# Fewer accumulating transfers and a re-ordered first step in a linear-attention and feed-forward kernel

## The chip, the core and the metric

The kernel runs on one core of a Trainium2 chip. The time is device microseconds of one execution, as a median over executions. The core has TensorE (matrix products into PSUM), VectorE, ScalarE and GpSimd (elementwise work), SyncE, which here only issues transfers, and 16 DMA engines that all queues share. SyncE's queue is SP in the profile, VectorE is DVE, GpSimd is POOL, ScalarE is ACT, TensorE is PE.

## What is computed

A gated linear attention over 4 sequences, 8 heads, 768 positions and head size 48, followed by a feed-forward layer (384 to 2048 to 384) with a piecewise quadratic activation:

```python
f = 1.0 / (1.0 + np.exp(-f_logit))
for t in range(S):
    state = f[:, :, t, :, None] * state + np.einsum('bhd,bhe->bhde', k[:, :, t], v[:, :, t])
    y[:, :, t] = np.einsum('bhd,bhde->bhe', q[:, :, t], state)
h = x @ w_in                    # x: y as 3072 tokens of 384
g = np.where(h >= 1, h, np.where(h <= -1, 0.0, (h + 1) ** 2 / 4))
out = g @ w_out
```

The weights arrive in double precision (`in_w`, two 32-bit words per number).

## The kernel before, in words

**Attention.** The 768 positions are cut into six steps of 128. In each step the eight heads are four pairs; pairs 0 to 2 fill 128 partitions together with a third each of pair 3's rows, so three tiles of keys, queries and gates are loaded and pair 3's tile is gathered from them by six moves (`move`, SBUF to SBUF, alternately issued by SP and ScalarE). `gate` turns the gate logits of one tile into running products: a sigmoid on ScalarE, then on VectorE two scans, a clamp (`end`), a reciprocal and two products with keys and queries, and a small product (`pf`, line 409) of 128x4 numbers, the decay of the state; GpSimd copies that on. For each pair, `scores` makes the products of keys and queries of four sequences in two PSUM banks; VectorE multiplies both banks with the causal mask (`am`, line 456); `outputs` multiplies with the values, and from step 1 on adds the state's part. ScalarE then copies the outputs in rounded form (`hi`, line 511), and VectorE writes what the rounding left (`lo`, line 512). Pair 3's outputs go by six moves (`x<-y`) into the tiles of pairs 0 to 2, since the feed-forward layer wants all 384 features of a position in three tiles. `transpose_tensor` turns the keys on TensorE, ScalarE copies them (`kn`, line 472), and `states` makes the step's part of the state. In steps 2 to 4 VectorE turns the keys instead (`transpose_rows`).

**Feed-forward.** 96 units: 16 slices of 128 hidden features for each of six steps. `unit_1` is nine matmuls (lines 204: three tiles, each with the weights' `lo` and `hi` times `x` hi, and `hi` times `x` lo), then ScalarE, ScalarE and VectorE for the activation (lines 208, 211, 216), ScalarE for its rounded part `ghi` (219), VectorE for the rest `glo` (222). `unit_2` is nine matmuls (228) into three banks that collect 16 units. TensorE's order is unit u+1's first product, then attention work if there is some, then unit u's second product.

**Weights.** 24 pieces of 128x512 (six per quarter: three of `w_in`, three of `w_out`; `k` numbers them). VectorE builds a float from the two words in three instructions (306, 309, 311). Then ScalarE writes the negative rounded value into `w_lo` (315), GpSimd issues a transfer that adds the exact value to it in SBUF (316, an accumulating transfer), and ScalarE writes `w_hi` (317). Units 0 to 3 need the first quarter, units 4 to 7 the second, and so on. Later 24 checks (325) load every piece once more.

**What sets the order.** The program lists operations with engine, estimated cost and dependencies (`Plan.add`); `Plan.order` is a list scheduler: each engine takes the ready operation with the earliest due time. TensorE's operations are chained in the order in which they are listed. The instructions are then written out in that order, and where the plan sees TensorE idle for over 700 ns it puts matmuls of zeros (`warm`, line 282) there. Each engine carries out its instructions in that fixed order. Transfers are given one of eight completion semaphores in turn, and an issue waits until the earlier transfer on its semaphore has landed.

Of the kernel before, what the change touches and what calls it, by code (L numbers as in the profile page):

```python
# [21 lines left out]
C = 128  # L22
NI = S // C
NP = H // 2
# [113 lines left out]
def gla_moe(ctx: ExitStack, tc: tile.TileContext, ff, kqd, f0, vv, wd, maskd, identd, gates, values, headsd, out):  # L138
# [8 lines left out]
    zeros = const.tile([128, 512], BF16, name="zeros")  # L147
# [5 lines left out]
    v = tiles(3, [C, B, 2, D], F32, "v")  # L153
# [18 lines left out]
    ident = const.tile([C, C], F32, name="ident")  # L172

# [14 lines left out]
    def whole(t):  # L188
        return t[:, 2 * N:]
# [89 lines left out]
    def warm(count):  # L279
        for _ in range(count):  # L280
            if opened["bank"] is not None:
                nc.tensor.matmul(opened["bank"], zeros[:, 0:128], zeros, start=opened["start"], stop=opened["start"])
# [14 lines left out]
    def split_piece(k):  # L297
# [69 lines left out]
    def gate(m):  # L367
# [41 lines left out]
        c["pf"] = [vec("small", lambda: nc.vector.tensor_tensor(out=whole(t), in0=et, in1=f0s[:, g:g + B], op=ALU.mult),  # L409
# [3 lines left out]
    def elementwise(n):  # L413
# [7 lines left out]
        c["lv"] = dma(v[n % 3], vv[i, p], 192, old(n - 3, "y", "st"))  # L421
# [18 lines left out]
    def scores(n):  # L440
# [11 lines left out]
        c["sc"] = add("PE", "scores", emit, c["kq"], [d for h in held for d in h[2]])  # L452
        c["am"] = []
# [8 lines left out]
    def transpose_tensor(n):  # L462
        i, p = pairs[n]
        c = att[n]
        b, ps, held = bank(i == 0)
# [21 lines left out]
    def outputs(n):  # L487
# [6 lines left out]

        def emit():
            for m in range(B):

                vb = v[n % 3][:, m].rearrange("u h e -> u (h e)")
                nc.tensor.matmul(ps[0:64, m], vb[:, 0:64], ms[0][:, m], start=True, stop=first)  # L499
                nc.tensor.matmul(ps[64:R, m], vb[:, D:], ms[1][:, m], start=True, stop=first)  # L500
# [5 lines left out]
        c["y"] = add("PE", "y0" if first else "y", emit, c["am"], c["lv"], c["db"], held)  # L506
# [5 lines left out]
        el = vec("dve", lambda: nc.vector.tensor_tensor(out=lo[:R], in0=yf[:R], in1=hi[:R].bitcast(F32), op=ALU.subtract), eh)  # L512
        banks[b] = [eh, el]
# [6 lines left out]
    def states(n):  # L520
# [4 lines left out]
        b, ps, held = bank(i == 0)  # L525
# [3 lines left out]
        def emit():  # L529
            for m in range(B):  # L530
                for h, (r, z) in enumerate(rows):
                    nc.tensor.matmul(ps[r:z, m, :D], kn[n % 2][:, B - 1 - m, r:z], v[n % 3][:, m, h], start=True, stop=True)
# [85 lines left out]

    for n in range(NP):
# [11 lines left out]
    BY_TENSOR = 2  # L631
# [7 lines left out]
    for u in range(NI * NJ):  # L639
        unit_1(u)  # L640
        for kind, n in sorted(groups.get(u, [])):
            if kind == 0:
# [3 lines left out]
                scores(n)  # L646
            else:
# [141 lines left out]
```

## Time and profile before

| | |
|---|---|
| median of 3 runs | 528.28 us (527.29 to 529.44) |
| profiled execution | 527.07 us, span of the program 525.3 us |
| TensorE busy | 500.1 us, 95% of the span, granted clock 0.986 |
| VectorE busy | 387.3 us, 74% |
| ScalarE busy | 243.6 us, 46% |
| GpSimd busy | 30.8 us, 6% |
| accumulating transfers (queue q0) | 24, 6.29 MB, 6.8% of the DMA engines' span |
| hardware queue of SP (q1) | 51.31 MB, 30.5% |

A busy TensorE in the profile is no TensorE at its peak, since matmuls overlap; nine matmuls of 128x512 that follow each other start over 2.04 us. The prediction reads the stages, the waits and the chain of waits; all times in it count from the span's start. A row of waits names the engine, its tile and line, and what ended its idle time.

### The profile page before, as it was taken

To read this page: it belongs to the slowest core of one execution; us is meant where nothing else is said; L and a number is where in the kernel's file an instruction comes from. 1 tells how busy PE (TensorE), PEld (TensorE's weight loads), DVE (VectorE), ACT (ScalarE), POOL (GpSimd) and SP (SyncE) were. 2 spreads that over 40 slices of the span, in tenths; PEclk is the share of its full clock that TensorE was granted. 3 is DMA by queue.
4 is the path that set the end of the run, shared out by engine and by line. 5 is a ranking of instruction groups with operands and counts; after the bars stand their busy time and mean duration, and the time that the engine had idled before them with its cause. 6 is when DMAs were issued, how large, how long until landed. Compare 5 with 4: busy or idle time off the path is not lost.

```text
span 525.3 us, 8288 instructions
## 1 busy us (share of the span) xinstructions
PE 500.1 (95%) x3226; PEld 404.0 (77%) x3226; DVE 387.3 (74%) x775; ACT 243.6 (46%) x399; POOL 30.8 (6%) x54
## 2 busy tenths in 40 slices
PE   8765998999999999999999999999999999999995
PEld 4433887788778888788888888888888888888883
DVE  7866998999999999898898798865655443433332
ACT  3334776664443544434434434534443544444542
POOL 1121221310000000000000000000000000000000
PEclk9996999999999999999999999999999999999998
DMA  8699988985311113322115423044542211100001
GB/s 297 211 294 243 242 226 221 281 203 134 109 51 55 35 62 87 119 103 100 60 57 132 129 72 116 23 148 119 176 131 92 80 41 31 61 1 0 1 0 66
DMA packets 24526, 60.57 MB, mean 115 GB/s; under 512 B 3744, under 2 KB 7328, under 8 KB 24480
## 3 DMA queue, kind: packets, MB, share of 16 engines
q1 hardware_dynamic: 19872, 51.31, 30.5%
q0 software_dynamic: 3456, 6.29, 6.8%
q10 hardware_dynamic: 1152, 2.37, 1.9%
q8 instruction: 27, 0.44, 0.3%
q14 instruction: 19, 0.16, 0.1%
HBM read 44.22 MB, written 4.72 MB: 93 GB/s over the span
## 4 chain that ended last, share of the span: by engine, by line
PE 71%; DVE 17%; DMA 7%; issue 2%; ACT 2%; ACTq 0%; SPq 0%; DVEq 0%
PE po L228 31%; PE ph L204 30%; DMA f<-in_f 3%; PE pa L450 3%; DMA x<-y 2%; PE pa L504 2%; PE pa L500 2%; DVE glo L222 2%; DVE kn L483 2%; DVE am L456 2%; DVE w L393 2%; DVE act L216 2%; DVE bits L311 1%; DVE f L400 1%; DMA raw<-in_w 1%
## 5 line engine op out<-in xcount | busy, mean ns | idle before, releaser
L204 PE MATMUL ph<-x,w_hi 128*128 128x512 f32 x576 | 179.1, 392 | 0.0
L208 ACT ACTIVATE act<-ph,half 128x512 f32<-128x512 f32 x96 | 66.0, 687 | 142.1 <-PE ph L204 136.1
L204 PEld LDWEIGHTS ph<-x,w_hi 128*128 128x128 f32 x576 | 109.4, 190 | 22.8
L204 PE MATMUL ph<-x,w_lo 128*128 128x512 f32 x288 | 113.3, 394 | 9.8 <-DMA x<-y 9.4
L228 PE MATMUL po<-ghi,w_lo 128*128 128x512 f32 x288 | 115.6, 401 | 1.3 <-ACT ghi L219 1.3
L216 DVE SCALAR_TENSOR_TENSOR act<-ph,act 128x512 f32<-128x512 f32 x96 | 65.8, 686 | 64.7 <-ACT act L211 63.6
L228 PE MATMUL po<-ghi,w_hi 128*128 128x512 f32 x288 | 112.4, 390 | 0.0
L219 ACT CAST ghi<-act 128x512 fp32r<-128x512 f32 x96 | 59.5, 620 | 81.7 <-DVE act L216 81.5
L228 PE MATMUL po<-glo,w_hi 128*128 128x512 f32 x288 | 83.3, 391 | 0.5 <-DVE glo L222 0.5
L222 DVE TENSOR_TENSOR glo<-act,ghi 128x512 fp32r<-128x512 f32 x96 | 65.9, 686 | 22.3 <-ACT ghi L219 21.2
L204 PEld LDWEIGHTS ph<-x,w_lo 128*128 128x128 f32 x288 | 54.7, 190 | 22.2 <-issue 9.9
L228 PEld LDWEIGHTS po<-ghi,w_lo 128*128 128x128 f32 x288 | 54.0, 188 | 15.2 <-ACT ghi L219 2.6
L228 PEld LDWEIGHTS po<-glo,w_hi 128*128 128x128 f32 x288 | 53.9, 188 | 13.2 <-DVE glo L222 1.8
L228 PEld LDWEIGHTS po<-ghi,w_hi 128*128 128x128 f32 x288 | 54.1, 188 | 10.4
L211 ACT ACTIVATE act<-act 128x512 f32<-128x512 f32 x96 | 60.7, 632 | 3.0
L483 DVE STREAM_TRANSPOSE kn<-kq 32x128 f32<-32x128 f32 x192 | 58.1, 303 | 2.9
L456 DVE TENSOR_TENSOR am<-pa,mask 128x512 f32<-128x512 f32 x43 | 29.3, 685 | 17.6 <-PE pa L450 13.9
L499 PE MATMUL pa<-am,v 128*64 128x128 f32 x184 | 35.5, 279 | 1.4 <-ACT kn L472 0.9
L500 PE MATMUL pa<-am,v 128*48 128x128 f32 x184 | 34.5, 277 | 0.5 <-DVE am L456 0.5
L503 PE MATMUL pa<-kq,dbd 112*64 112x128 f32 x160 | 30.6, 272 | 0.0
L504 PE MATMUL pa<-kq,dbd 112*48 112x128 f32 x160 | 30.6, 272 | 0.0
L450 PEld LDWEIGHTS pa<-kq 48*128 48x128 f32 x344 | 21.3, 187 | 6.6 <-issue 4.9
(79 smaller groups left out, 454.4 us busy)
## 6 DMA issues: line engine op xcount, KB each, us to landing
raw<-in_w SPq DMA_DIRECT2D x48, 512.0 KB, 3.7
kq<-in_kq SPq DMA_DIRECT2D x18, 512.0 KB, 4.2
w_lo<-bits POOLq DMA_DIRECT2D x24, 256.0 KB, 6.9
v<-in_v SPq DMA_DIRECT2D x24, 192.0 KB, 4.3
out_y<-raw SPq DMA_DIRECT2D x18, 256.0 KB, 2.3
f<-in_f SPq DMA_DIRECT2D x16, 256.5 KB, 3.0
kq<-kq SPq DMA_DIRECT2D x18, 64.2 KB, 3.3
kq<-kq ACTq DMA_DIRECT2D x18, 64.2 KB, 3.5
```

The source lines that it names most:

```text
L204: nc.tensor.matmul(ps, w_in(part, j, kt), xt[:, kt, t], start=(n == 0), stop=(n == 8))
L208: nc.scalar.activation(a, ps, AF.Relu, bias=half, scale=0.5)
L211: nc.scalar.activation(a, a, AF.Square)
L216: nc.vector.scalar_tensor_tensor(out=a, in0=ps, scalar=1.0, in1=a, op0=ALU.max, op1=ALU.min)
L219: nc.scalar.copy(hi, a)
L222: nc.vector.tensor_tensor(out=lo, in0=a, in1=hi.bitcast(F32), op=ALU.subtract)
L228: nc.tensor.matmul(po[e], w_out(part, j, e), g, start=(j == 0 and n == 0), stop=(j == NJ - 1 and n == 2))
L450: nc.tensor.matmul(ps[:, b], kt[a:z, B - 1 - b], qt[a:z, b], start=True, stop=True)
L456: o = vec("dve", lambda t=t, ps=ps: nc.vector.tensor_tensor(out=t, in0=ps, in1=mask.rearrange("u (o t) -> u o t", o=1).broadcast_to([C, B, ...
L483: nc.vector.transpose(kn[n % 2][u:u + 32, :, r:r + 32], src[:, :, u:u + 32])
L500: nc.tensor.matmul(ps[64:R, m], vb[:, D:], ms[1][:, m], start=True, stop=first)
L504: nc.tensor.matmul(ps[64:R, m], dt[:, m, 64:R], qt[:, m], start=False, stop=True)
```

## The change

1. *Weights.* Only pieces with odd `k` from 7 on (nine) are still made by an accumulating transfer. For the other fifteen ScalarE writes `w_hi` first and VectorE subtracts it from the value (new line 323).
2. *Step 0.* Scores of the next pair are listed ahead of a pair's outputs, and the masks (`masks`) apart from the scores. All outputs come ahead of the turned keys: pairs 0 and 1 are turned after the last remainder, pairs 2 and 3 after unit 1 (lines 480, 564). 
3. *Step 0's remainders.* Each output product is made in two banks (lines 514 and 521); a matmul with a negative unit matrix (`minus`, line 540) subtracts the rounded copy from the second one, and ScalarE writes the remainder from there (541). VectorE's instruction stays for steps 1 to 5 (544 and 545).
4. *Decays.* The small product `pf` is GpSimd's (415).
5. *Fillers and costs.* Ahead of unit 0 the zero matmuls fill the whole planned gap and four more are added; the tile of zeros is 128x128 and read four times; some planning costs differ; the values have four buffers instead of three.

```diff
-HOP, LANDING, PER_KB, NEAR = 200, 2000, 3.0, 2000
-COST = dict(mm=227, scores=1100, y0=1050, y=1850, states=500, turn=500, rows=317, scan=1145, dve=605, small=200, state=365,
-            words=430, act=710, copy=530, sig=540, issue=480, near=600, least=300, swdge=1000)
+HOP, LANDING, PER_KB, NEAR = 200, 2000, 3.0, 2700
+COST = dict(mm=227, scores=1100, y0=1850, y=1850, states=500, turn=500, rows=317, scan=1145, dve=605, small=200, state=365,
+            words=390, act=710, copy=530, sig=540, issue=480, near=600, least=300, swdge=900)
...
-        n = sca("copy", lambda: nc.scalar.activation(w_lo[:, c], val, AF.Copy, scale=-1.0), v)
-        l = add("POOL", "swdge", lambda: nc.gpsimd.dma_start(w_lo[:, c], val, accum_op=ALU.add), n, near=True)
-        h = sca("copy", lambda: nc.scalar.copy(w_hi[:, c], val), v)
+        if k >= 6 and k % 2:
+
+            n = sca("copy", lambda: nc.scalar.activation(w_lo[:, c], val, AF.Copy, scale=-1.0), v)
+            l = add("POOL", "swdge", lambda: nc.gpsimd.dma_start(w_lo[:, c], val, accum_op=ALU.add), n, kb=560)
+            h = sca("copy", lambda: nc.scalar.copy(w_hi[:, c], val), v)
+        else:
+            h = sca("copy", lambda: nc.scalar.copy(w_hi[:, c], val), v)
+            l = vec("dve", lambda: nc.vector.tensor_tensor(out=w_lo[:, c], in0=val, in1=w_hi[:, c].bitcast(F32), op=ALU.subtract), h)
...
-        c["pf"] = [vec("small", lambda: nc.vector.tensor_tensor(out=whole(t), in0=et, in1=f0s[:, g:g + B], op=ALU.mult),
+        c["pf"] = [add("POOL", "least", lambda: nc.gpsimd.tensor_tensor(out=whole(t), in0=et, in1=f0s[:, g:g + B], op=ALU.mult),
...
+        again = bank(True) if first else None
...
+                else:
+                    for r, z, a, t in ((0, 64, 0, ms[0]), (64, R, D, ms[1])):
+                        nc.tensor.matmul(again[1][r:z, m], vb[:, a:a + z - r], t[:, m], start=m == 0, stop=False)
...
-        el = vec("dve", lambda: nc.vector.tensor_tensor(out=lo[:R], in0=yf[:R], in1=hi[:R].bitcast(F32), op=ALU.subtract), eh)
-        banks[b] = [eh, el]
+        c["rest"] = b, again, yf[:R], hi[:R], lo[:R], eh
+        if not first:
+            remainder(n)
+
+    def remainder(n):
+
+        i, p = pairs[n]
+        b, again, yf, hi, lo, eh = att[n]["rest"]
+        xt = x[i % 2]
+        if again:
+            y = wide(again[1])[:R]
+            o = add("PE", 300, lambda: nc.tensor.matmul(y, minus, hi, start=False, stop=True), eh, ready["minus"])
+            el = sca("act", lambda: nc.scalar.copy(lo, y), o)
+            banks[b], banks[again[0]] = [eh], [el]
+        else:
+            el = vec("dve", lambda: nc.vector.tensor_tensor(out=lo, in0=yf, in1=hi.bitcast(F32), op=ALU.subtract), eh)
+            banks[b] = [eh, el]
...
     for n in range(NP):
         prepare(n)
-        if n == 0:
-            ready["ident"] = dma(ident, identd, 64)
         scores(n)
-        outputs(n)
-        transpose_tensor(n)
-        states(n)
+        if n > 0:
+            outputs(n - 1)
+        if n > 1:
+            remainder(n - 2)
+        masks(n)
+    outputs(NP - 1)
+    remainder(NP - 2)
+    remainder(NP - 1)
+    for n in (0, 1):
+        transpose_tensor(n, True)
+    for n in (0, 1):
+        states(n, True)
...
     for u in range(NI * NJ):
         unit_1(u)
+        if u == 1:
+            for n in (2, 3):
+                transpose_tensor(n)
+            for n in (2, 3):
+                states(n)
...
-                if idle and o.start - idle > 700:
+                if o is unit_in[0, 0]:
+
+                    warm(int((o.start - idle) / 230) + 4)
+                elif idle and o.start - idle > 700:
```

TensorE at the end of step 0 and ahead of unit 0, before (`kq_71` holds pair 3's keys, `kn` turned keys, `ph` the units' banks):

```order
L500 MATMUL po_118<-am_79,v_72 48x128
L469 MATMUL pa_111<-ident,kq_71 128x112 x4
L282 LDWEIGHTS zeros
...
L532 MATMUL pa_112<-v_72,kn_82 64x48
...
L282 MATMUL ph_115<-zeros 128x512
L204 MATMUL ph_114<-x_88,w_lo 128x512
```

and with the change (`y_91` holds pair 3's rounded outputs):

```order
L521 MATMUL po_118<-am_79,v_75 64x128
...
L540 MATMUL po_118<-y_91,minus 112x512
L480 MATMUL po_119<-ident,kq_68 128x112 x4
L480 MATMUL po_120<-ident,kq_69 128x112 x4
...
L564 MATMUL pa_114<-v_73,kn_83 48x48
...
L283 MATMUL ph_117<-zeros 128x512
L205 MATMUL ph_116<-x_89,w_lo 128x512
```

Pairs 0 and 1 are now turned where pair 3 was, behind the last remainder; ten zero matmuls stood between the states and unit 0, and eleven do now.

SP around the moves of pair 3's outputs, before (`raw` are pieces of the weights):

```order
L241 DMA kq_69<-in_kq 128x1024
L241 DMA raw_95<-in_w 128x512
L241 DMA kq_70<-in_kq 128x1024
L241 DMA raw_96<-in_w 128x512
L241 DMA raw_97<-in_w 128x512
L241 DMA v_74<-in_v 128x384
L241 DMA raw_95<-in_w 128x512
L241 DMA v_72<-in_v 128x384
L246 DMA x_88<-y_90 16x1024 x3
```

and with the change:

```order
L242 DMA raw_96<-in_w 128x512
L242 DMA raw_97<-in_w 128x512
L242 DMA raw_98<-in_w 128x512
L242 DMA raw_96<-in_w 128x512
L242 DMA kq_68<-in_kq 128x1024
L247 DMA x_89<-y_91 16x1024 x3
L242 DMA raw_97<-in_w 128x512
L242 DMA kq_69<-in_kq 128x1024
```

Two of step 1's three loads of keys and queries, and its values, now stand behind the moves; seven pieces of the weights stand ahead of them in both.

VectorE ahead of unit 6's third activation step, before:

```order
L311 SCALAR_TENSOR_TENSOR bits_100<-raw_97,bits_100 128x512
L396 TENSOR_SCALAR end_77<-w 128x4
L399 RECIPROCAL rec<-end_77 128x4
L400 SCALAR_TENSOR_TENSOR f_66<-f_66,rec 128x512
L402 TENSOR_TENSOR kq_70<-kq_70,w 128x512
L404 TENSOR_TENSOR kq_70<-kq_70,f_66 128x512
L456 TENSOR_TENSOR am_80<-pa_112,mask 128x512
L512 TENSOR_TENSOR x_89<-pa_113,x_89 112x512
L216 SCALAR_TENSOR_TENSOR act_86<-ph_114,act_86 128x512
```

and with the change:

```order
L313 SCALAR_TENSOR_TENSOR bits_101<-raw_98,bits_101 128x512
L399 SCALAR_TENSOR_TENSOR w<-f_66,ones 128x512
L323 TENSOR_TENSOR w_lo<-bits_99,w_hi 128x512
L323 TENSOR_TENSOR w_lo<-bits_101,w_hi 128x512
L402 TENSOR_SCALAR end_78<-w 128x4
L405 RECIPROCAL rec<-end_78 128x4
L406 SCALAR_TENSOR_TENSOR f_66<-f_66,rec 128x512
L217 SCALAR_TENSOR_TENSOR act_87<-ph_116,act_87 128x512
```

The two products and the mask have moved behind the step, and two of the new weight remainders stand ahead of it. From the start to this step VectorE's list has 15 pieces in both, 11 weight remainders instead of none, no output remainders instead of 5, 11 masks instead of 12, 8 wide key and query products instead of 10, and no decays instead of 4.

More of the change, by code (lines that the diff above doesn't have):

```diff
@@ L145, in tiles @@
         return [const.tile(shape, dtype, name=f"{name}_{k}") for k in range(count)]
-    zeros = const.tile([128, 512], BF16, name="zeros")
+    zeros = const.tile([128, 128], BF16, name="zeros")
     ones = const.tile([128, B, C], F32, name="ones")
@@ L152, in gla_moe @@
     kq = tiles(NP, [128, 2 * N + B], F32, "kq")
-    v = tiles(3, [C, B, 2, D], F32, "v")
+    v = tiles(4, [C, B, 2, D], F32, "v")
     w = const.tile([128, B, C], F32, name="w")
@@ L172, in gla_moe @@
     ident = const.tile([C, C], F32, name="ident")
+    minus = const.tile([R, R], F32R, name="minus")
     f0s = const.tile([128, NI * NT * B], F32, name="f0s")
@@ L281, in warm @@
             if opened["bank"] is not None:
-                nc.tensor.matmul(opened["bank"], zeros[:, 0:128], zeros, start=opened["start"], stop=opened["start"])
+                nc.tensor.matmul(opened["bank"], zeros, zeros.rearrange("p (o c) -> p o c", o=1).broadcast_to([128, 4, 128]),
+                                 start=opened["start"], stop=opened["start"])
     add("PE", 4000, lambda: warm(12), set_zeros)
@@ L420, in elementwise @@
                 gate(m)
[L421 removed]
+        c["lv"] = dma(v[n % 4], vv[i, p], 192, old(n - 4, "y", "st"))
         if p == NP - 1:
@@ L452, in scores, with masks @@
         c["sc"] = add("PE", "scores", emit, c["kq"], [d for h in held for d in h[2]])
+        c["held"] = held
+    def masks(n):
+        c = att[n]
+        held = c["held"]
         c["am"] = []
@@ L493, in outputs @@
         qt, dt = part(kq[p], 1)[:R], dbd[n % 2]
+        again = bank(True) if first else None
         def emit():
             for m in range(B):
[L498 to L500 removed]
+                vb = v[n % 4][:, m].rearrange("u h e -> u (h e)")
+                for r, z, a, t in ((0, 64, 0, ms[0]), (64, R, D, ms[1])):
+                    nc.tensor.matmul(ps[r:z, m], vb[:, a:a + z - r], t[:, m], start=True, stop=first)
                 if not first:
@@ L504, in emit @@
                     nc.tensor.matmul(ps[64:R, m], dt[:, m, 64:R], qt[:, m], start=False, stop=True)
-        c["y"] = add("PE", "y0" if first else "y", emit, c["am"], c["lv"], c["db"], held)
+                else:
+                    for r, z, a, t in ((0, 64, 0, ms[0]), (64, R, D, ms[1])):
+                        nc.tensor.matmul(again[1][r:z, m], vb[:, a:a + z - r], t[:, m], start=m == 0, stop=False)
+        c["y"] = add("PE", "y0" if first else "y", emit, c["am"], c["lv"], c["db"], held, again and again[2])
         xt = x[i % 2]
@@ L518, in outputs, with states @@
                         for t in range(NT) for k, (r, z) in enumerate(((48, 0), (112, 64)))]
-    def states(n):
+    def states(n, early=False):
         i, p = pairs[n]
@@ L524, in states @@
             return
-        b, ps, held = bank(i == 0)
+        b, ps, held = bank(early)
         rows = HEADS if i > 0 else ((0, 64), (64, R))
@@ L531, in emit @@
                 for h, (r, z) in enumerate(rows):
-                    nc.tensor.matmul(ps[r:z, m, :D], kn[n % 2][:, B - 1 - m, r:z], v[n % 3][:, m, h], start=True, stop=True)
+                    nc.tensor.matmul(ps[r:z, m, :D], kn[n % 2][:, B - 1 - m, r:z], v[n % 4][:, m, h], start=True, stop=True)
         c["st"] = add("PE", "states", emit, c["kn"], c["lv"], held)
@@ L646, in gla_moe @@
                 scores(n)
+                masks(n)
             else:
```

8 lines of the change are left out of this document (5 added, 3 removed).

## The prediction, made before the changed kernel was timed

> **What bounds the kernel now.** I read the stages first, then TensorE's waits, then the chain of waits where TensorE is idle. The columns are busy time (and instructions) of TensorE, its weight load, VectorE, ScalarE and GpSimd, then granted clock, share of the DMA engines, GB/s.
>
> ```profile
> 0.00:34.01 34.01, 28.09 (x255) 16.21 (x256) 29.33 (x58) 14.09 (x28) 7.68 (x19) 1.00 0.82 265
> 34.01:44.72 10.71, 1.26 (x7) 0.43 (x5) 4.93 (x10) 2.18 (x4) 1.72 (x2) 0.77 1.02 253
> 44.72:52.89 8.17, 6.88 (x19) 5.11 (x19) 5.78 (x10) 3.71 (x7) 0.86 (x1) 0.67 0.98 261
> 52.89:81.39 28.50, 28.50 (x188) 23.80 (x189) 27.50 (x50) 20.78 (x37) 7.29 (x9) 1.00 0.92 239
> 81.39:150.00 68.61, 66.69 (x488) 54.73 (x488) 64.97 (x133) 38.82 (x66) 9.31 (x13) 1.00 0.67 177
> 150.00:360.00 210.00, 209.75 (x1403) 172.89 (x1401) 184.31 (x407) 91.62 (x145) 3.98 (x10) 1.00 0.27 85
> ```
> ```profile
> PE ph L204 <- DMA x<-y: 9.4, 1, 9.4
> ```
> ```profile
> 34.01 10.57 DMA x<-y
> 44.72 6.90 PE ph L204 x18
> 52.89 2.32 PE po L228 x9
> 55.21 2.04 PE ph L204 x9
> ```
>
> From 52.89 us on TensorE hardly stops: 1.9 us idle up to 150, 0.25 in the next 210. So all that can be won lies before. TensorE waits 9.4 us for the six moves of pair 3's outputs into the tiles of step 0, then runs its first 18 matmuls in 6.90 us, where a warm nine take 2.04 (4.08 for 18): the clock shows 0.77 and 0.67 there. A second limit stands close behind. From 52.89 to 81.39 VectorE is busy 27.5 of 28.5 us; starting TensorE earlier does not start VectorE's work earlier. Both must be worked out, and the later one decides.
>
> **Limit 1: the moves.** They are issued at 34.01, when VectorE has written pair 3's remainder, and land last 10.57 us later, against a median of 3.1 for the later steps:
>
> ```profile
> 28.79 1.26 DVE L456 TENSOR_TENSOR am<-po,mask 128x512 f32<-128x512 f32 x2
> 31.22 0.59 ACT L511 CAST y<-po 112x512 fp32r<-112x512 f32 x1 [2.10 <-PE po L500]
> 33.31 0.67 DVE L512 TENSOR_TENSOR y<-po,y 112x512 fp32r<-112x512 f32 x1
> 34.01 4.98 SPq L246 DMA_DIRECT2D x<-y  x3
> 34.01 7.43 ACTq L246 DMA_DIRECT2D x<-y  x3
> ```
> ```profile
> DMA to landing us min/median/max: 2.2/3.1/4.6
> ```
> ```profile
> 20.27 0.69 DVE L512 TENSOR_TENSOR x<-pa,x 112x512 fp32r<-112x512 f32 x1 [1.53 <-ACT x L511]
> 27.66 1.22 DVE L393 TENSOR_TENSOR_SCAN w<-f,ones 128x512 f32<-128x512 f32 x1
> 30.59 0.27 PE L500 MATMUL po<-am,v 128*48 128x128 f32 x1
> 30.70 0.27 PE L500 MATMUL po<-am,v 128*48 128x128 f32 x1
> ```
>
> *Issue.* Two masks take 1.26 us where one takes 0.67 or so: an added wide VectorE instruction costs 0.60. The second mask of pair 3 starts at 28.79 + 0.60 = 29.4. In the new order VectorE has, ahead of it, three remainders fewer (-1.8), step 1's first scan no longer (-1.2), three small decays fewer (-0.45), one weight remainder more (+0.6): -2.8, so 26.6, ending 27.2. The 1.53 us wait for a cast also falls; I keep it as reserve, as step 0's second half now has more on ScalarE. The outputs are 16 records on TensorE, now 32 (each product is made in two banks), and a pair of records starts every 0.11 us: done about 2 us after the mask, 29.2. Cast (0.59), one matmul into the second bank (about 0.45 with its drain, taken from the 0.39 of one row), second cast (0.59): moves issued at about 30.9 instead of 34.0. The remainder so leaves VectorE's queue, where at 33.31 it stood behind a piece's words and a scan. What it waits for now is ScalarE's cast, and behind that matmul on TensorE stand the turns of pairs 0 and 1. One of these in turn holds SP: the load of step 1's first keys waits for pair 0's turn, and SP's three moves stand behind that load. The turn comes right behind the last remainder matmul (near 30.3, and 0.6 long), so the load goes out at 30.9, with the moves; that costs SP's moves one issue, 0.4.
>
> *Landing.* What the moves queue behind is told by the DMA view of 25 to 45 us (packets, MB, share of 16 engines):
>
> ```profile
> q1 hardware_dynamic: 1252, 3.74, 58.5%
> q0 software_dynamic: 681, 1.26, 34.7%
> ```
> ```profile
> raw<-in_w SPq DMA_DIRECT2D x6, 512.0 KB, 7.6
> w_lo<-bits POOLq DMA_DIRECT2D x6, 256.0 KB, 9.8
> ```
>
> Accumulating transfers took 0.347 x 20 = 6.9 us of all engines for 1.26 MB, 5.5 us per MB; the loads 11.7 us for 3.74 MB, 3.1 per MB. Four accumulations were issued ahead of the moves (1.05 MB): -5.8 us of engine time. SP's order also leaves two loads of keys and three of values behind them (2 x 0.52 + 3 x 0.20 = 1.6 MB): -5.1. Together 10.9, against a delay over the median of 10.57 - 3.1 = 7.5; issuing 3.1 earlier takes back 3.1. The backlog is gone by this count, except that weights' piece 6 and step 1's first keys now stand right ahead on SP (1.05 MB, 3.2 us). So landing takes 3.1 to 6.3; I take 5.5: 36.4.
>
> *TensorE beside it.* ScalarE now issues its three moves ahead of two turned-key copies.
>
> ```profile
> 31.12 0.60 PE L469 MATMUL pa<-ident,kq 112*128 112x112 f32 x4
> 31.75 0.53 ACT L472 COPY kn<-pa 128x448 f32<-128x448 f32 x1
> 32.34 0.67 PE L532 MATMUL pa<-v,kn 128*64 128x48 f32 x16 [0.19 <-ACT kn L472]
> 32.94 2.33 PE L282 MATMUL ph<-zeros 128*128 128x512 bf16 x10
> ```
>
> Issuing at 0.5 each ends at 32.4, two copies at 33.5, the second states at 34.4, then eleven zero matmuls (0.23 each, 2.5): 36.9. So unit 0 starts at about 36.9 by this queue and 36.4 by the moves, and warm. Then 4.08 for 18 matmuls and 2.4 for pairs 2 and 3's turns and states (0.5 and 0.67 each), which fill what was a wait of 1.3 for ScalarE. The first output matmuls come at 43.4 instead of 52.89: **9.5 us** is what limit 1 allows. If this cover is gone (the hi of unit 0 late), those 2.4 us are simply added.
>
> **Limit 2: VectorE.** I take the tightest place, unit 6's third activation step, which fixes TensorE's second product of unit 6:
>
> ```profile
> 3.45 1.27 DVE L393 TENSOR_TENSOR_SCAN w<-f,ones 128x256 f32<-128x256 f32 x2 [1.63 <-ACT f L391]
> 81.39 0.68 DVE L216 SCALAR_TENSOR_TENSOR act<-ph,act 128x512 f32<-128x512 f32 x1
> ```
> ```profile
> 83.26 0.39 PE L228 MATMUL po<-ghi,w_lo 128*128 128x512 f32 x1
> ```
> ```profile
> L219 ACT CAST ghi<-act 128x512 fp32r<-128x512 f32 x96 | 59.5, 620 | 81.7 <-DVE act L216 81.5
> L409 DVE TENSOR_TENSOR kq<-end,f0s 128x4 f32<-128x4 f32 x18 | 2.7, 152 | 0.1
> ```
>
> Up to 81.39 VectorE was busy 29.33 + 4.93 + 5.78 + 27.50 = 67.5 and idle 13.9. Up to the same step the new order has eleven weight remainders more, five output remainders, one mask and two key products fewer, four decays fewer: 3 x 0.60 - 4 x 0.15 = +1.2. So the step can start at 68.7 + X, X being the idle time, and the product 1.4 later (0.68, and ScalarE's 0.62). Against 83.26 the gain is at most 83.26 - 70.1 - X = 13.1 - X. X is the unknown. At least the start up to 3.45 remains (2.6), and the 1.0 of the last stage: 3.6. At most nothing is recovered: 13.9. The large parts, 5.8 us idle in 34.01:44.72 and 2.4 in the next stage, are waits for weights behind the same backlog, so I am near the low end: 3.6, 0.7 as otherwise in 3.45 to 34 us, and 1.2 for one late load: X = 5.5, **7.6 us**. It is less than limit 1, so VectorE decides.
>
> **What else the edits cost.** Decays on GpSimd: 18 x 0.15 leave VectorE, and their readers wait for GpSimd's queue:
>
> ```profile
> L411 POOL COPY f0s<-kq x18: 186/279/1182, 14.0 to 348.4; 128x4 f32<-128x4 f32 x18
> 10.20 0.25 ACT L383 ACTIVATE f0s<-f0s 128x72 f32<-128x72 f32 x1
> DMA to landing us min/median/max: 3.5/6.9/11.6
> ```
>
> A copy of that size takes 0.28, the first 1.18. Gate 2's clamp on VectorE (about 14.2 in the new order) waits for the first decay, which can start at 10.45; with 1.18 for it nothing is late. The fourth values' buffer, the smaller tile of zeros and the negative unit matrix cost no engine of the path anything: their loads and the one ScalarE pass lie in the first 15 us, ahead of the first cast. Three more zero matmuls stand ahead of unit 16 (0.6); TensorE idled 1.9 us in that stage, so I charge half of them and as much again for late pieces. The nine accumulations left (k = 7 to 23, odd) land 6.9 after issue; fifteen ScalarE negations fall (0.63 each) where ScalarE had room. Sum: -7.6 + 0.6 = **-7.0 us**. The profiled execution took 527.07 with a span of 525.3; 518.3 and 520.1 are its counterparts. The median of the three runs, 528.28, becomes **521.3**.
>
> **Rivals.**
>
> *TensorE alone decides.* If X is 3.6, limit 1 rules: -9.5, and up to 1.9 us of idle after 52.89 closes: 517 to 519. For it: weights wait less. Against: VectorE would need to be packed from the first microsecond.
>
> *GpSimd is late at its first multiply.* Past 14.2 us each microsecond goes into X, as the clamp, and all behind it on VectorE, waits. Ending 2.5 us late, it leaves 4.5: 523.8. For it: the order puts a separate GpSimd instruction ahead of the first multiply, and the first copy took four times the median. [...]
>
> *A remaining accumulation holds TensorE.* Unit 8 needs piece 13. VectorE finishes its words six us of work ahead of unit 6's third step (68.7 + 5.5 = 74.2), so at 68; negated and issued near 70.5, it lands at 77.4 by the median and at 82.1 by the maximum of 11.6, against a unit 8 at 78.3 (83.26 + 2.04 - 7.0). The gain falls to about 3: 525 to 526, no change to be told.
>
> *Slower.* The fifteen remainders (9 us of VectorE) arrive, the relief does not: if VectorE's idle stays at 13.9 because SP's loads still wait for one another, the step at unit 6 comes 0.8 later than before, and by unit 16 fifteen weight remainders (9.0) against four output remainders (2.4) and nine decays (1.3) make 5.3 us more work, half of which TensorE's attention groups may cover: 528.3 + 2.7 = 531. It decides once X passes 13.1.
>
> **How the numbers follow.** VectorE decides, 4.5 to 9 us: 0.50. TensorE alone: 0.17. GpSimd late: 0.12, of which all but the edge is faster. Accumulation or late loads, within 2.6 us: 0.13. Slower: 0.08. What 0.5% is, 2.6 us, is about what runs of this kernel can tell. So faster 0.79, same 0.13, slower 0.08. The range leaves out the far ends of both last cases: 516.5 to 527.5; the likeliest case alone, 519.3 to 523.8.
>
> **What would show it.** In the new profile: the moves issued at 31 and landing within 6.3 us; unit 0 at 36 to 38, with the granted clock near 1.00; TensorE waiting again, a few us in all, for the hi and lo parts of units 0 to 7; VectorE's idle to unit 6 at 4 to 7 us. Wrong would be: moves still landing 10 us after issue; a VectorE wait for GpSimd in step 0; or a TensorE wait for accumulating transfers.

## The result, and the profile after

The changed kernel takes 521.31 us (median of four executions, 519.36 to 521.77) against 528.52 for the kernel before on the same chip (527.29 to 529.44): a ratio of 0.985, with an interval of 0.983 to 0.988, so 7.2 us faster. The profiled execution took 519.36 us with a span of 517.3. It was the fastest of the four, about 2 us under the median, which matters below when traces are compared. The experiments ran on several chips, each beside the kernel before, which took 528.56 to 529.26 us there; so medians less than 1 us apart are not told apart, and the ratios compare better.

The stages of the changed kernel, with the columns of the prediction's first fence, cut where its own start is:

```profile
30.00:40.00 10.00, 6.38 (x58) 3.70 (x57) 8.26 (x15) 3.35 (x8) 1.31 (x2) 1.00 0.87 238
40.00:50.00 10.00, 9.33 (x75) 7.70 (x74) 9.58 (x16) 7.58 (x15) 1.02 (x1) 1.00 1.01 302
50.00:75.00 25.00, 24.91 (x174) 20.84 (x173) 24.54 (x44) 15.71 (x27) 5.03 (x7) 1.00 0.80 230
75.00:150.00 75.00, 73.86 (x522) 60.63 (x521) 72.75 (x147) 40.10 (x67) 8.89 (x12) 1.00 0.51 142
```

Before, TensorE was idle for 9.4 us in one piece and ran its first units at a clock of 0.67 to 0.77. Now the clock is 1.00 in each stage shown, from 30 to 150 us, and TensorE is busy nearly throughout from 40. VectorE is as full as TensorE: 8.26 of 10, 9.58 of 10, 24.54 of 25, 72.75 of 75. TensorE's waits of the whole changed kernel, the four largest after the start:

```profile
PE ph L205 <- DMA x<-y: 2.4, 1, 2.4
PE pa L564 <- ACT kn L483: 1.9, 2, 1.2
PE pa L456 <- DVE kq L410: 1.6, 2, 1.2
PE po L229 <- DMA w_lo<-bits: 0.8, 1, 0.8
```

The moves are still what it waits for longest, 2.4 instead of 9.4 us. The timeline of the three engines there:

```profile
30.22 1.80 ACTq L247 DMA_DIRECT2D x<-y  x3
30.64 0.33 SPq L242 DMA_DIRECT2D raw<-in_w  x1
31.06 0.43 SPq L242 DMA_DIRECT2D kq<-in_kq  x1
31.58 1.99 SPq L247 DMA_DIRECT2D x<-y  x3
38.65 0.50 PE L205 MATMUL ph<-x,w_lo 128*128 128x512 f32 x1 [2.39 <-DMA x<-y]
45.54 0.50 PE L229 MATMUL po<-ghi,w_lo 128*128 128x512 f32 x1
```
```profile
DMA to landing us min/median/max: 6.2/6.6/7.0
```

ScalarE's three leave at 30.2, SP's at 31.6 to 33.0, behind two loads of 0.52 MB, and these three land 6.2 to 7.0 us after issue (the last row). Unit 0 starts at 38.65 instead of 44.72, the first output matmul at 45.54 instead of 52.89: 7.35 us, about the gain of the whole. The chain of waits from 30 us on does not go through the moves but through the weights:

```profile
30.64 4.41 DMA raw<-in_w
35.08 0.03 issue
35.11 5.12 DMA raw<-in_w
40.28 0.04 issue
40.32 0.44 DVE bits L308
```

Piece 6 leaves at 30.64, piece 7 only when it has landed, and VectorE's words of piece 7 start at 40.32. The chain then stays on VectorE. VectorE's whole work up to unit 6's third activation step, and then up to unit 15's, stands in two rows (third number after the comma: VectorE):

```profile
0.00:75.11 75.11, 67.10 (x538) 49.32 (x539) 68.73 (x125) 37.73 (x69) 13.15 (x28) 0.98 0.82 248
...
0.00:122.97 122.97, 113.81 (x890) 87.95 (x891) 115.67 (x210) 66.02 (x117) 20.62 (x37) 0.99 0.75 218
```

Up to unit 6 it is idle for 75.11 - 68.73 = 6.4 us, where the kernel before had 13.8. What went away is its wait for the loads of the weights, here before (up to unit 6's third step at 81.39) and with the change:

```profile
DVE bits L306 <- DMA raw<-in_w: 8.1, 4, 2.3
```
```profile
DVE bits L308 <- DMA raw<-in_w: 1.0, 1, 1.0
```

So by this one trace two chains end within a microsecond of each other, and it does not say which one sets the time.

### The profile page after: what moved, and what is told of

It is laid out like the page before. It is cut to its first block, busy times and chain, and to the rows that moved or that the text cites. A ratio compares the mean times of both kernels' runs of the same rounds, so it can differ in the third digit from the quotient of the medians.

```text
span 517.3 us, 8421 instructions
## 1 busy us (share of the span) xinstructions
PE 501.5 (97%) x3295; PEld 407.0 (79%) x3295; DVE 390.6 (76%) x768; ACT 238.8 (46%) x389; POOL 31.0 (6%) x57
## 4 chain that ended last, share of the span: by engine, by line
PE 76%; DVE 17%; DMA 4%; issue 1%; ACT 0%; SPq 0%; ACTq 0%; DVEq 0%
PE po L229 33%; PE ph L205 31%; PE pa L456 4%; PE pa L514 3%; DVE kn L494 3%; PE pa L518 3%; DMA raw<-in_w 2%; DVE glo L223 2%; DVE bits L313 2%; DVE bits L311 2%; DVE act L217 1%; DMA v<-in_v 1%; DVE am L467 1%; DVE w L399 1%; DVE w_lo L323 1%
## 5 line engine op out<-in xcount | busy, mean ns | idle before, releaser
L205 PEld LDWEIGHTS ph<-x,w_hi 128*128 128x128 f32 x576 | 108.1, 188 | 22.5
L467 DVE TENSOR_TENSOR am<-pa,mask 128x512 f32<-128x512 f32 x45 | 30.7, 686 | 17.1 <-PE pa L456 13.8
L514 PE MATMUL pa<-am,v 128*48 128x128 f32 (+1 forms) x368 | 36.8, 277 | 0.1
L456 PEld LDWEIGHTS pa<-kq 48*128 48x128 f32 x360 | 22.4, 188 | 8.9 <-issue 5.3
L456 PE MATMUL pa<-kq 48*128 48x128 f32 x360 | 27.0, 285 | 1.6 <-DVE kq L410 1.6
```

What stands on the lines that cost most here:

```text
L205: nc.tensor.matmul(ps, w_in(part, j, kt), xt[:, kt, t], start=(n == 0), stop=(n == 8))
L456: nc.tensor.matmul(ps[:, b], kt[a:z, B - 1 - b], qt[a:z, b], start=True, stop=True)
L467: o = vec("dve", lambda t=t, ps=ps: nc.vector.tensor_tensor(out=t, in0=ps, in1=mask.rearrange("u (o t) -> u o t", o=1).broadcast_to([C, B, ...
L514: nc.tensor.matmul(ps[r:z, m], vb[:, a:a + z - r], t[:, m], start=True, stop=first)
```

## The experiments

Three theories. V, the prediction's: VectorE decides, and earlier moves gain nothing. M: the landing of the moves decides, since TensorE has hardly any idle time behind it. P: both are at par, and only relief of both is worth its whole amount. One measure is the row above: VectorE's busy and idle time up to unit 15's third step. Where VectorE is the floor, its idle time stays at the least it can have; where TensorE is, the idle time grows. The other is when TensorE reaches the first output matmul, unit 3 and unit 15.

**Step 0's moves left out.**

```diff
             moved[i] = [move(k, ...) for t in range(NT) for k, (r, z) in enumerate(((48, 0), (112, 64)))]
+            if i == 0:
+                for o in moved[i]:
+                    o.emit = lambda: None
```

> The changed kernel with step 0's six moves left out (rows 112 to 127 of step 0's input are zeros, set by GpSimd in the first 6 us, so those rows of step 0's outputs are wrong; all else, the order of every engine too, is that of the change). TensorE then waits for nothing of the moves: unit 0 can start when its own queue is done, near 36.3 us instead of 38.65. Theory M (the moves' landing decides): every later unit moves with it, the whole gains about 2.3 us, 519.0 where the change has 521.3, and unit 9 starts near 84.4 instead of 86.70. Theory V (VectorE decides, the prediction's): unit 0 early, but TensorE waits 2.3 us more for the hi and lo of units 0 to 7, unit 6's third activation step stays at 75.1, the time stays within 0.5 of 521.3. Theory P (both at par): part of it, 0.5 to 1.5, the rest seen as new waits for VectorE.

Measured: 519.84 us (517.99 to 520.41), ratio 0.983 (0.9805 to 0.9855) to the kernel before; 1.5 below the change, with intervals that overlap. Unit 0 starts at 36.18, although step 0 itself ended 1.6 us later in this execution: TensorE waited 2.8 us for a product of keys where the change shows 1.2, and its granted clock up to 40 us was 0.91 where the change has 0.96. And yet the first output matmul comes at 45.12, 0.4 earlier only. What holds it, in the timeline of ScalarE and in TensorE's waits of this kernel:

```profile
41.86 0.63 ACT L319 ACTIVATE w_lo<-bits 128x512 fp32r<-128x512 f32 x1 [1.87 <-DVE bits L314]
...
43.48 0.95 ACT L484 COPY kn<-pa 128x448 f32<-128x448 f32 x2
```
```profile
PE pa L568 <- ACT kn L484: 2.7, 1, 2.7
```
```profile
0.00:123.89 123.89, 116.38 (x895) 91.30 (x896) 116.67 (x210) 66.46 (x117) 23.62 (x38) 0.96 0.72 214
```

The turned keys' copies of pairs 2 and 3 stand on ScalarE behind piece 7's negation, and that waits for piece 7's words. VectorE itself works without a gap from 36.0 to 45 here, so it is its own work ahead of these words that holds them, and its idle time up to unit 15 stays at 7.2 us. After TensorE's wait the clock is also lower: 0.95 from 40 to 75 us, where the change has 1.00, and the four matmuls from 45.76 on take 0.63 us each instead of 0.40, so unit 2 starts at 48.74 instead of 47.72. The time itself lies only 0.8 above what M said, so it is the trace that speaks against M: without the moves another wait holds the first output matmul almost as long, and the moves alone gain nothing that is clearly told.

**A lighter VectorE.**

```diff
             out=t, in0=hw, scalar=0xC0000000, in1=t, op0=ALU.bitwise_and, op1=ALU.bitwise_or), v)
+        if k < 12:
+            v.emit = lambda: None
         piece.append(v)
```

> The changed kernel with the third of the three word instructions left out for the first 12 weight pieces: 12 x 0.60 = 7.2 us less on VectorE before unit 6's third activation step (the sign bit of those weights is lost, so the outputs are other numbers; all else stays). Theory M: TensorE, which idles 0.1 us from 50 to 75 and 1.1 from 75 to 150, has nothing to gain: 521.3, at most 1 less. Theory V: VectorE's steps come up to 7 us earlier and the end at least 2 us earlier: 519 or less. Theory P: 521.3, as under M, since the moves then decide alone.

Measured: 518.26 us (516.81 to 519.90), ratio 0.981 (0.978 to 0.983): 3.0 less than the change by the medians, as V has it, though the intervals touch. The row of stages up to unit 15's third step:

```profile
0.00:122.53 122.53, 115.65 (x895) 89.65 (x896) 109.41 (x197) 65.83 (x117) 20.87 (x37) 0.97 0.75 220
```

VectorE has 6.3 us less to do, and the step comes only 0.4 sooner: its idle time has grown from 7.3 to 13.1, as P and M have it, and unit 0 stands at 38.41 for the moves. In the traces the gain is 1.1 at the end. Unit 15 starts only 0.5 sooner, and the rest comes at unit 15, where this kernel does not wait for the last accumulating transfer. The medians' 3.0 differ from it by about what the change's profiled execution lies under its median.

**Both.** The two edits together.

> Both edits in one: step 0's moves left out and the third word instruction left out for the first 12 pieces. Theory M: as with the moves alone, 519.0. Theory V: as with the lighter VectorE alone. Theory P: about 2.3 less than the change, 519.0, where each edit alone gives 1.5 or less.

Measured: 515.10 us (514.28 to 515.49), ratio 0.975 (0.972 to 0.977): 6.2 less than the change, more than the two apart (1.5 and 3.0), and more than any theory had. The medians' surplus of 1.7 is about what the spread of the runs leaves open; the traces tell it more clearly.

```profile
0.00:118.97 118.97, 114.01 (x894) 88.56 (x894) 109.73 (x197) 65.82 (x117) 22.31 (x38) 0.99 0.75 223
```

Unit 0 starts at 34.68, and unit 15's step comes 4.0 us sooner than in the change, where each edit alone left it within 0.9 of 122.97. When TensorE starts what (us):

| | unit 0 | first output | unit 3 | unit 15 | unit 16 |
|---|---|---|---|---|---|
| the change | 38.65 | 45.54 | 53.51 | 118.82 | 124.50 |
| no moves | 36.18 | 45.12 | 54.69 | 119.69 | 124.25 |
| lighter VectorE | 38.41 | 45.49 | 53.49 | 118.34 | 122.90 |
| both | 34.68 | 41.95 | 49.91 | 115.02 | 119.58 |

At the first output matmul the edits gain 0.4 and 0.05 apart and 3.6 together. That is P: two limits side by side. From unit 3 to unit 15 all four take 64.9 to 65.3 us, and TensorE is busy for 64.9 of the change's 65.3: there TensorE's own work sets the pace, and what was won by unit 3 is carried on. P's sum was too small, since it took the moves for 2.3: leaving them out also spares ScalarE the 1.8 us of issuing three of them, so that it copies the first turned keys at 30.16 instead of 32.06, and TensorE's own queue reaches unit 0 at 34.68.

**No zero matmuls ahead of unit 0.**

```diff
-                    warm(int((o.start - idle) / 230) + 4)
+                    warm(0)
```

> The changed kernel without the eleven zero matmuls ahead of unit 0: TensorE idles about 4.9 us (33.7 to 38.65) ahead of unit 0. The kernel before idled 9.4 us there and needed 6.90 us for 18 matmuls at a granted clock of 0.67 to 0.77, against 4.08 warm. Theory M: the clock falls in part, the 18 matmuls take 4.08 to 6.9, and the time grows by as much: 0 to 2.8 us, I take 1.4 (522.7). Theory V: the 18 matmuls take longer but the end does not move by more than 0.5.

Measured: 520.53 us (519.57 to 522.19), ratio 0.986 (0.983 to 0.988): no difference to the change, as V has it. TensorE does run slower, as its timeline shows after its 4.4 us of waiting:

```profile
38.37 0.79 PE L205 MATMUL ph<-x,w_lo 128*128 128x512 f32 x1 [4.41 <-DMA x<-y]
...
42.08 0.39 PE L205 MATMUL ph<-x,w_lo 128*128 128x512 f32 x1
```

The first nine matmuls take 3.71 us instead of 2.18, the second nine are warm (a start every 0.41 us up to 42.08, every 0.23 behind it), and unit 2 starts 1.23 later. At unit 15 it is still 0.96 behind, at unit 16 nothing of it is left (124.34 against 124.50): the change waits at unit 15 for the last accumulating transfer, 0.82 us, and for what follows it, and this execution does not. So a loss of 1 us up to unit 15 is seen in the trace, and none in the time.

**The parts, one undone or alone.** First all 24 pieces by accumulating transfers again, the rest of the change kept.

```diff
-        if k >= 6 and k % 2:
+        if True:
```

> The weights part of the change undone, all else kept (its order planned anew): all 24 pieces' remainders come by accumulating transfers, none by VectorE. VectorE has 9 us less to do, the queues 1.05 MB of accumulations more ahead of the moves. Theory W (the weights part carries the gain, by the landing of the moves, as the prediction has it): the moves are issued near 30 but land some 10 us later, unit 0 near 40 to 41, the time 523 to 526. Theory O (the order of step 0 carries it, the accumulations weigh little): unit 0 by 39, and with VectorE lighter no more than 521.3.

Measured: 533.43 us (532.35 to 535.09), ratio 1.008 (1.0055 to 1.011): slower than the kernel before, and 12 slower than the change. The DMA view of 22 to 42 us, VectorE's waits up to 80 us and the row up to unit 15's step:

```profile
q0 software_dynamic: 635, 1.17, 36.2%
```
```profile
DVE bits L308 <- DMA w_lo<-bits: 1.7, 1, 1.7
```
```profile
0.00:140.34 140.34, 126.18 (x926) 96.61 (x927) 123.34 (x236) 73.80 (x133) 33.82 (x54) 0.94 0.82 225
```

The moves are issued at 31.6 to 34.2 and land 5.6 to 8.4 later, unit 0 starts at 41.46, and VectorE's idle time up to unit 15 is 17.0 us, as before the change (131.71 with 114.77 busy, 16.9). Up to unit 6's step it is idle 15.7 us, more than the kernel before. Theory W (523 to 526) is right in direction and far too small: 1.17 MB of accumulations take 36% of all engines for 20 us, and the buffers of the words come free only when they land.

The weights' part alone, in the kernel before:

```diff
+        if k >= 6 and k % 2:
             n = sca("copy", lambda: nc.scalar.activation(w_lo[:, c], val, AF.Copy, scale=-1.0), v)
...
+        else:
+            h = sca("copy", lambda: nc.scalar.copy(w_hi[:, c], val), v)
+            l = vec("dve", lambda: nc.vector.tensor_tensor(out=w_lo[:, c], in0=val, in1=w_hi[:, c].bitcast(F32), op=ALU.subtract), h)
```

> The kernel before with the weights part alone: nine accumulations, fifteen remainders on VectorE, step 0's order, its remainders and the decays as before. Theory W: the moves, issued at 34 or a little later, land within 6 us, unit 0 near 40 and cold in part, first output matmul near 47: some 5 to 6 us less than before, 522.5 to 523.5. Theory O: VectorE's 9 us more are paid in full and nothing lands sooner to effect: 527 to 530.

Measured: 526.05 us (524.89 to 527.25), ratio 0.995 (0.993 to 0.997): 3.2 less than before, between the two theories (522.5 to 523.5 and 527 to 530). Here the moves, issued at 34.5, land within 2.7 us, unit 0 starts at 37.20 and unit 2 at 46.09, sooner than in the whole change. It is lost again: unit 10 starts at 94.53 instead of 90.78. TensorE's wait ahead of it, and the row up to unit 15's step:

```profile
92.36 0.47 PE L228 MATMUL po<-ghi,w_lo 128*128 128x512 f32 x1 [1.59 <-ACT act L211]
```
```profile
0.00:126.84 126.84, 114.30 (x829) 84.97 (x835) 118.84 (x220) 63.58 (x112) 13.69 (x27) 0.99 0.69 210
```

VectorE has 3.2 us more to do than in the change (step 0's remainders and the decays among it) and is idle 8.0, hardly more than there: so VectorE holds this kernel back, although TensorE started sooner. The weights' part frees the queue, and the other parts free the VectorE time that it costs; alone it gains 3.2, they without it lose 4, together they gain 7.2.

The decays on VectorE again, and step 0's remainders on VectorE again:

```diff
-        c["pf"] = [add("POOL", "least", lambda: nc.gpsimd.tensor_tensor(
+        c["pf"] = [vec("small", lambda: nc.vector.tensor_tensor(
```

> The changed kernel with the products of the gates' ends and first gates (18 small ones) on VectorE again, as before the change: 18 x 0.15 us more on VectorE, of it 4 to 7 of them (0.6 to 1.0 us) ahead of unit 6's third step. By the prediction's sum: 0.6 us slower at most, 521.3 to 521.9. If GpSimd was late at its first product (the rival): 1 to 2.5 us faster, 519 to 520.

```diff
-        again = bank(True) if first else None
+        again = None
```

> The changed kernel with step 0's four remainders on VectorE again (no second bank, no unit matrix with -1; planned anew, which also puts the moves on SyncE's queue ahead of two of the weights' loads that stand ahead of them in the change). By the prediction's sum four remainders of 0.60 us each return to VectorE: the moves are issued up to 1 us later or earlier, VectorE has 2.4 us more up to unit 6: if VectorE's amount of work decides, 2.4 us slower, 523.7. If the moves' landing decides, they land sooner, unit 0 starts at 36.5 to 37.5 and the time is 519 to 520.5.

Measured: 523.29 us (522.93 to 524.38), ratio 0.989 (0.987 to 0.990), for the first, and 525.98 (523.83 to 527.26), ratio 0.9925 (0.990 to 0.995), for the second: 2 and 4 to 5 slower than the change, more than the 0 to 0.6 and 2.4 expected; the first one's interval touches the change's. Up to unit 15's third step, first the one and then the other:

```profile
0.00:127.14 127.14, 117.53 (x896) 90.90 (x896) 117.03 (x215) 65.65 (x117) 12.06 (x27) 0.96 0.71 211
```
```profile
0.00:130.77 130.77, 116.98 (x836) 88.15 (x837) 119.06 (x214) 63.40 (x113) 18.95 (x37) 0.95 0.70 206
```

VectorE's work grows by 1.4 and 3.4 us, its idle time by 2.8 and 4.4. The planner put other orders around the edit (in the first the moves leave 2.2 us later), and in both TensorE waits 2.6 us in one piece and has a lower clock around it (0.83 and 0.88 from 40 to 50 us, the change 1.00); how the second part of each loss divides among these is not shown. In the second the moves leave at 29.5, and unit 0 still starts at 38.54, since they land 7.6 to 9.0 later: three loads of 0.52 MB leave right ahead of them.

```profile
28.16 0.33 SPq L242 DMA_DIRECT2D kq<-in_kq  x1
28.54 0.90 SPq L242 DMA_DIRECT2D raw<-in_w  x2
```

Neither gave the gain that a late GpSimd or a pure limit by the moves would have given.

**Moves by another queue, or first.** Both keep the change's order otherwise; in the second, `late` holds the loads of piece 6 and of step 1's first keys.

```diff
+            if i == 0:
+                for o, (t, (r, z)) in zip(moved[0][0::2], [(t, (48, 0)) for t in range(NT)]):
+                    o.emit = lambda t=t, r=r, z=z: nc.gpsimd.dma_start(xt[r:r + 16, t]..., y3[z + 16 * t:z + 16 * t + 16]...)
```

> The changed kernel, in its own order, with the three of step 0's moves that SyncE issues (31.6 to 33.0, behind two loads of 0.52 MB) issued by GpSimd, idle then, on its own queue; SyncE's loads behind them go up to 2 us sooner. Each of GpSimd's issues took 0.86 to 1.02 us: 30.3 to 33. Theory P (moves and weights' loads limit at par): both limits are relieved, unit 0 near 36.5, the turned keys of pairs 2 and 3 not held by piece 7's negation, the time 1.5 to 2.3 less than the change, 519 to 520. Theory M (moves alone): the same start, the same time. Theory V (VectorE's amount of work alone): unit 0 earlier, the time at 521.3.

```diff
-        for o in plan.order():
+        ops = [o for o in plan.order() if o not in late]
+        k = max(ops.index(o) for o in moved[0])
+        for o in ops[:k + 1] + late + ops[k + 1:]:
```

> The changed kernel, in its own order, with SyncE's three moves put ahead of the two loads (weights' piece 6, step 1's first keys) that stand right ahead of them: the moves leave 0.9 us sooner with 1.05 MB less in front, the two loads up to 2 us later. Theory M: landing falls from 6.4 to 3 or so, unit 0 near 36.3, 2.3 less: 519. Theory P: unit 0 near 36.3, but piece 6, 7 and the keys come later, VectorE idles 1 to 2 us more ahead of unit 6, and TensorE waits for it or for ScalarE's queue behind it: 520.5 to 522.5.

Measured: 519.21 us (518.74 to 519.33), ratio 0.982 (0.979 to 0.984), with GpSimd's moves; 520.29 (519.38 to 521.61), ratio 0.984 (0.982 to 0.987), with the moves first. For the latter, the landing of SP's and ScalarE's moves, TensorE's wait and ScalarE's row:

```profile
DMA to landing us min/median/max: 2.2/2.6/2.8
```
```profile
PE pa L569 <- ACT kn L488: 4.1, 2, 2.6
```
```profile
43.19 0.63 ACT L321 ACTIVATE w_lo<-bits 128x512 fp32r<-128x512 f32 x1 [1.80 <-DVE bits L316]
```

The two loads ahead are worth 4 us of landing (2.6 against 6.6). Unit 0 no longer waits for the moves at all (37.58, after a step 0 that here ended 1.4 us later, again behind a long wait for a product of keys, 2.4), but piece 7's words come later, and ScalarE's queue behind them: P's case. The 2.6 us wait is again followed by slower matmuls, 0.63 us each at 47.57 and 47.99. GpSimd's moves land no sooner than SP's did, though no load is on GpSimd's queue; TensorE starts unit 0 and stops inside it for the next tile:

```profile
DMA to landing us min/median/max: 4.9/6.9/6.9
```
```profile
38.14 0.47 PE L205 MATMUL ph<-x,w_lo 128*128 128x512 f32 x1 [1.26 <-issue]
```

The two loads leave at 30.57 and 30.99, among GpSimd's three moves. What the own queue gains is the earlier issue, since nothing is put back: unit 0 starts at 35.84, the first output matmul at 44.95 instead of 45.54, and TensorE's largest single wait becomes the last accumulating transfer at unit 15:

```profile
PE po L229 <- DMA w_lo<-bits: 2.0, 1, 2.0
```
```profile
0.00:122.43 122.43, 113.59 (x889) 87.67 (x889) 115.73 (x210) 66.10 (x117) 22.00 (x40) 0.99 0.74 219
```

VectorE's idle time is down to 6.7 us, the least seen with this amount of work. The gain of 2.1 is one of medians alone: the profiled executions took 519.33 and, for the change, 519.36.

**Three edits in one**, GpSimd's moves, piece 7 behind unit 0's hi, the last piece by VectorE:

> The edit with GpSimd's moves, and two more in the same order: piece 7's negation, rounding and accumulation put behind unit 0's hi on ScalarE's queue (so that the turned keys of pairs 2 and 3 don't stand behind piece 7's words), and the last accumulating transfer (piece 23, for which TensorE waited 0.82 us at unit 15) made by VectorE instead (0.60). Theory P: about 1 less than with GpSimd's moves alone, 518 to 519. Theory M: no difference to GpSimd's moves alone but the 0.8 at unit 15.

Measured: 518.92 us (518.61 to 520.31), ratio 0.982 (0.980 to 0.985), the lowest of the kernels that compute the whole reference, though not to be told from GpSimd's moves alone, and from the change itself only by medians 2.4 apart. TensorE reaches unit 16 at 122.82 instead of 124.50, and unit 23 only 0.6 sooner. Unit 15's third step is no sooner than in the change, with VectorE idle for 6.7:

```profile
0.00:123.03 123.03, 114.97 (x898) 88.21 (x899) 116.31 (x211) 65.65 (x116) 21.21 (x39) 1.00 0.72 217
```

**Remainders on GpSimd**, on top of these:

```diff
+            if k >= 3:
+                l.emit = lambda: nc.gpsimd.tensor_tensor(out=w_lo[:, c], in0=val, in1=w_hi[:, c].bitcast(F32), op=ALU.subtract)
```

> The edit with GpSimd's moves, the late piece 7 and the last piece by VectorE, and besides eleven of VectorE's weight remainders (pieces 3 to 5 and the even ones from 6 on) subtracted by GpSimd, which is idle there: 11 x 0.60 = 6.6 us less on VectorE up to unit 14, five of them (3.0 us) ahead of unit 6's third step. No row shows what a 128x512 subtraction takes on GpSimd; at up to 3 us each, none is late for its unit. Theory P (VectorE's work is one of two limits at par, the other relieved here already): 1.5 to 3 less than the three edits alone, 516 to 517.5. Theory M: 518.9 as without. [...]

(They are twelve, not eleven.) Measured: 521.23 us (520.72 to 522.79), ratio 0.987 (0.985 to 0.989): 2.3 slower than without. GpSimd needs 1.3 to 1.7 us for one, so none is late. But VectorE's row grows though it has twelve instructions fewer than the 211 of the kernel without:

```profile
0.00:125.02 125.02, 115.54 (x895) 87.88 (x896) 119.70 (x199) 65.37 (x116) 38.29 (x51) 1.00 0.72 213
```

Which of its instructions grew is in the last section. This is the clearest row for VectorE as one of the two floors: its idle time falls to 5.3, its busy time rises by 3.4, and the time with it. From unit 3 to unit 15 it takes 68.6 us, where the change and the seven other edits that keep its order nearly whole take 64.9 to 65.5: VectorE lies so close behind TensorE there that 6.3 us less for it gain 0.5, and 3.4 more lose 3.1.

## Why the prediction was right or wrong

- *The time*, 521.3 forecast and measured. That it was hit to the tenth is partly luck: the runs spread over 2.4 us, the traces differ by 7.7, and the terms were less good than the sum.
- *Issue of the moves*, 30.9: ScalarE's left at 30.22, SP's at 31.58 to 33.0. Right for the first, too early for SP's, where two loads stood ahead and the three go out 0.6 apart.
- *Landing*, 3.1 to 6.3, taken as 5.5, for 36.4: this is the term that was mis-sized. It was counted from 30.9 for all six; SP's left 0.7 and more later and landed 6.2 to 7.0 after that. So unit 0 came at 38.65, not at 36.9, though TensorE's own queue was ready at 36.26. That the older backlog would be gone was right; the weight of the 1.05 MB right ahead was named and taken too light, as 3.2 us: put behind, landing is 2.6 instead of 6.6, so it is 4.
- *Limit 1*, 9.5 us: 7.35 at the first output matmul. The 1.75 by which unit 0 came later and 0.4 more between unit 0 and the first output matmul (6.89 instead of 6.48, with a wait of 0.67 for ScalarE's copy of turned keys in it) make the difference of 2.15. The warm clock came as forecast (18 matmuls in 4.2 us); without zero matmuls 1.2 us are lost there, of which the whole time shows nothing.
- *Limit 2*, X = 5.5, VectorE's work 68.7, unit 6's third step at 74.2: 6.4, 68.73 and 75.11. Right within 1 us, and by the mechanism named: VectorE's waits for loads of the weights fell from 8.1 to 1.0 us. Unit 6's second product starts at 76.48 instead of 83.26, 6.8 us sooner where 7.6 were forecast.
- *"VectorE decides"*: half right. A lighter VectorE gave 3.0 and no moves 1.5 or nothing, but both 6.2: limit 1, mis-sized by 2.1, had come down to limit 2, and the two are at par up to the first output matmul. The sign that was named, TensorE waiting a few us in all for the hi and lo parts of units 0 to 7, did not come: from the first output matmul to unit 15 it waits 0.3 us for such a part, and its own work sets the pace. The forecast time was right because the lower of the two limits was well sized; that the other came out no lower was luck.
- *The edits' 0.6*: three zero matmuls and a late piece around unit 15 to 16 cost 1.6 us there: unit 15 takes 5.68, a plain unit 4.08, and one with the zero matmuls and no such wait 4.56 (no moves, lighter VectorE, both). So 0.5 are the zero matmuls and 1.1 the late piece, with TensorE's wait of 0.82 for the last accumulating transfer. That wait was named as a sign of being wrong, and the rival of a remaining accumulation appears in it, but small, 0 to 2 us in the traces, and at unit 15 and piece 23 instead of unit 8 and piece 13.
- *GpSimd late*: fell. Its first product took 0.62 us at 9.67, the second 0.39, VectorE never waits for it, and with the products back on VectorE the kernel is slower. No run shows the 2.5 us late that this rival was counted with: the first product, ahead of which GpSimd stood idle for 6.55 us waiting for ScalarE, ended at 10.29, and gate 2's clamp began at 14.39. The first copy's fourfold time, which spoke for it, does not go with being first: with the change the first copy takes 0.30, the median one 1.11 (below).
- *Slower*: half of its mechanism is seen. With all accumulations kept X does not fall (15.7 up to unit 6, before 13.8), and the kernel takes 533.4, without the fifteen remainders that this rival counted. Taking fifteen accumulations away is what makes the rest pay.

Open stays why the medians of the lighter VectorE gain 3.0 where its trace gains 1.1: the change's other executions, about 2 us longer than its profiled one, have no trace. The last accumulating transfer is one candidate (waits of 0, 0.8 and 2.0 us in three traces), but the kernel without it was not faster by more than the measurement tells. The new order of step 0 was never undone by itself, so what it gains alone is not shown.

## What to carry to other kernels

Work out each limit by itself up to the same instruction, and ask of every relief where the next limit stands: here two reliefs of 0.4 and 0.05 us at the first output matmul made 3.6 together, and 1.5 and 3.0 of the whole time made 6.2. A small transfer for which an engine waits should not be issued right behind large loads, on SP's queue or beside them on GpSimd's: with no load right ahead the moves landed after 2.2 to 2.8 us, with 1.05 MB after 4.9 to 7.0, with 1.57 MB after 7.6 to 9.0, an estimate of 4 us per MB from these. What is put behind in turn needs its own count. An engine that shows 6% busy is not free of cost for another: twelve subtractions moved to GpSimd made VectorE's row up to unit 15 3.4 us longer here. Look at the other engine's instruction times before and after work is moved.

## What the hardware showed beside

VectorE's and GpSimd's instructions take longer side by side, in the rows that follow. In the kernel with remainders on GpSimd, its rows and VectorE's in the same microseconds:

```profile
33.21 2.80 POOL L331 TENSOR_TENSOR w_lo<-bits,w_hi 128x512 fp32r<-128x512 f32 x2 [1.45 <-ACT w_hi L328]
```
```profile
33.45 1.43 DVE L309 TENSOR_SCALAR bits<-raw 128x512 uint32<-128x512 uint32 x1
34.92 1.64 DVE L312 SCALAR_TENSOR_TENSOR bits<-raw,bits 128x512 uint32<-128x512 uint32 x1
36.60 0.69 DVE L314 SCALAR_TENSOR_TENSOR bits<-raw,bits 128x512 uint32<-128x512 uint32 x1
```

In the kernel of the three edits, where VectorE makes these remainders, VectorE's first takes 0.42 on average and the others 0.69; with the remainders on GpSimd the averages are 0.50, 0.75 and 0.80. The two subtractions take 1.4 each, and VectorE's first two instructions end 0.3 and 0.55 after them: as if each had waited for the end of one and then run. The other way round, in the changed kernel, GpSimd's copy of 128x4 numbers beside VectorE's scan:

```profile
14.79 1.23 DVE L406 TENSOR_TENSOR_SCAN act<-act,rec 128x512 f32<-128x512 f32 x1
```
```profile
14.89 1.11 POOL L417 COPY f0s<-kq 128x4 f32<-128x4 f32 x1
```

It starts 0.10 into the scan and ends with it, at 16.0, where the shortest of its 18 copies takes 0.19; their median is 1.11. Thirteen of them lie beside such a scan and take 1.11 to 1.21, the five beside other instructions 0.19 to 0.53. The kernel before shows 1.18 for the first of them, beside a remainder and a product of VectorE (13.84 to 15.13). What makes the two engines slow beside each other, no run here shows. A second thing: after 4.4 us without a matmul, nine matmuls took 3.71 us and the next nine 2.05; after 9.4 us, in the kernel before, 18 took 6.90. After waits of 2.65 and 2.59 us (no moves, moves first) matmuls of 0.63 us each follow, from 45.76 and 47.57 on; after the change's wait of 2.39 nine took 2.18, and the clock is 1.00 from 30 to 50 us.
